# Decoding feed-forward weights in an attention stage: four half tiles in every chunk, and v^T e placed behind the scores

## The chip, the cores and the metric

One core of one Trainium2 chip runs the whole program. The metric is the device time of one execution in microseconds (us); the time of a kernel is the median of its runs. The core's engines are named as the profile names them: PE (TensorE matmuls), PEld (TensorE weight loads), DVE (VectorE), ACT (ScalarE), POOL (GpSimd) and SP (the queue that issues the transfers here).

## The reference

Three stages follow one another; 4 batches, 8 heads, 576 positions, head size 64, so 2304 rows of width 512.

```python
scores = scale * q @ k^T                       # 576 x 576 per head
scores = where(scores >= max(scores) - tau, scores, -1e9)
attn = exp(scores - max) / (sum + 1e-9)
x = (attn @ v), heads side by side             # 2304 x 512
h = ((x @ w1) * (x @ w2)) @ w3 @ w_out         # first feed-forward block
g = h @ w_in;  out = max(0.01 * g, g) @ w_out2 # second feed-forward block
```

q, k and v are float32. The weights are float64: the chip gets each as two 32-bit words and has to make float32 values of them, which is called decoding here.

## The kernel before

**Attention.** A unit is a pair of heads and one of two groups of query rows (256 rows or 320 rows). There are 32 units, in the order batch, group, pair. A unit of the first group has two chunks (128 query rows for both heads), one of the second group has three; the first of those three, written `None`, has 64 rows of both heads packed into one tile and counts with weight 1, all others with weight 2. That makes 80 chunks, `STEPS`, n = 0 to 79. Batch 0 group 0 is n = 0 to 7, batch 0 group 1 is n = 8 to 19.

One turn of the main loop (line 454 on) does, for chunk n: `mask(n)` (L239, DVE multiplies the exponentials by "score is over the threshold", two heads, and reads the one `sc` tile in PSUM); `scores(n + 1)` (L213 or L217 on PE into that same tile, then L223 maximum on DVE and L225 exponential on ACT, one head after the other); `transposes(n)` (L259 and L270 on PE, copied into `HH` by ACT at L274 and by DVE at L272, the last 64 keys into a tail tile `tl` by ACT at L277). In the first chunk of a unit `weighted` runs v^T e of the unit before (L292, 20 matmuls, from `tl` first and then from `HH`, copied out by ACT at L295); in the second `normalise` scales it (L320 and L322 on PE).

**Filling PE.** Between these pieces the loop puts matmuls of other work: `fill(0)`, `fill(1)` and `fill(2)` each run a share of `filler` (the first feed-forward block of a batch and group that is already done, `gated`, groups of 12 matmuls, L381 and L400) and at most one half of a fold. `fold_weights` multiplies w3 by w_out once, in 16 half folds of 4 column sums (L359). A half fold may only run when the weights that it reads have been decoded before this chunk began: `8 + 2 * (folded // 2) + 2 <= decoded`. At n = 9 the loop turns to `gated` for batch 0 group 0: it runs what is left of the folds at once, and `filler` is busy from n = 10 on.

**Decoding.** `stream` loads and decodes the weights in halves of a tile (128 x 512 words). There are 40 of them for the attention stage: 8 of `wo`, 16 of `w3` and 16 of `w12` (the matrices of `gated`). A half takes two ACT instructions (L142 and L144, each pinned behind the ACT instruction traced before it), a shift on DVE (L145) and a sum on POOL (L148). A half of `w12` takes more: the ACT copy at L150, the sum at L151 and a difference at L153, every second one on DVE, the rest on POOL. The temporaries `t` and `lw` have two buffers each, `w3` has three tiles in use at a time, and `raw`, the loaded words, four.

`load_halves(k)` decodes the next k halves. Each chunk takes 1.2 halves per unit of weight, collected in `due_halves` (2 or 3 in a chunk of weight 2). Half of them are called behind `fill(0)`, the others at the end of the chunk. `gated` calls `load_halves(1)` for itself when a matrix that it needs is not there.

**Order.** PE and SP keep the order of the program. The order of DVE, ACT and POOL is chosen when the program is built, from a model of the times, except for the pinned instructions. So the place of a call in the loop sets PE's and SP's order, and for the others only what is wanted first.

```python
        fill(0)                        # L474
        load_halves(kh // 2)
        if weigh:
            weighted(*weigh.pop())
        pieces = transposes(n)
```

Of the kernel before, what the change touches and what calls it, by code (L numbers as in the profile page):

```python
# [39 lines left out]
def attention_gated_ffn(ctx: ExitStack, tc: tile.TileContext, qkv, tau, w3t, wout, w12, w2, out):  # L40
# [144 lines left out]
    def scale_unit(u):  # L185

        if u >= len(units):
            return
        g = units[u][1]
        qk = qk_t[u]  # L190
        q = qk[:, S:S + GROUPS[g][1]]
        tc.keep_in_program_order(
            nc.vector.tensor_scalar(out=q, in0=q, scalar1=scl, scalar2=None, op0=ALU.mult))
        if g:
            for a in range(2):
                o = a * D
                nc.gpsimd.tensor_copy(qz[u % 2][o:o + D, o:o + D], qk[o:o + D, S:S + D])
# [4 lines left out]
    def scores(n):  # L202

        pair, g, c = STEPS[n]
        u = units.index((pair, g))
        qk = qk_t[u]
        heads = range(1 if c is None else 2)
        sc = ps_a.tile([P, 2, 2, 512], F32, tag="sc", name="sc")
        for half in range(2):
            ks = slice(half * HS, half * HS + HS)  # L210
            for a in heads:
                if c is None:
                    nc.tensor.matmul(sc[:, a, half, :HS], qz[u % 2], qk[:, ks], start=True, stop=True)  # L213
                else:
                    r = slice(a * D, a * D + D)
                    o = S + Q0[c] - GROUPS[g][0]
                    nc.tensor.matmul(sc[:, a, half, :HS], qk[r, o:o + P], qk[r, ks], start=True, stop=True)  # L217
        e = apool.tile([P, 2, S], F32, tag="e", name="e", bufs=2)
        ths = []
        for a in heads:  # L220
            nm = apool.tile([P, 1], F32, tag="nm", name="nm", bufs=4)
            th = apool.tile([P, 1], F32, tag="th", name="th", bufs=4)
            nc.vector.tensor_reduce(out=nm, in_=sc[:, a, :, :HS], op=ALU.max, axis=AX.XY, negate=True)  # L223
            nc.vector.tensor_scalar(out=th, in0=nm, scalar1=-1.0, scalar2=cb, op0=ALU.mult, op1=ALU.add)
            nc.scalar.activation(  # L225
                e[:, a].rearrange("p (a b) -> p a b", a=2), sc[:, a, :, :HS], AF.Exp, bias=nm)
            ths.append(th)
        sc_t[n], e_t[n] = (sc, ths), e

    def mask(n):  # L230
        pair, g, c = STEPS[n]
        sc, ths = sc_t.pop(n)
        key = (pair, g)
        if key not in stat:
            stat[key] = apool.tile([P, 5], F32, tag="stat", name="stat", bufs=4)
        for a, th in enumerate(ths):
            ev = e_t[n][:, a].rearrange("p (a b) -> p a b", a=2)
            o = 4 if c is None else 2 * (c % 2) + a
            nc.vector.scalar_tensor_tensor(  # L239
                out=ev, in0=sc[:, a, :, :HS], scalar=th, in1=ev, op0=ALU.is_ge, op1=ALU.mult,  # L240
                accum_out=stat[key][:, o:o + 1])
# [3 lines left out]
    def transposes(n):  # L245

        pair, g, c = STEPS[n]  # L250
        if (pair, g) not in he_t:
            he_t[pair, g] = apool.tile([P, 4, 2, 320], F32, tag="HH", name="HH")
        HH, tail = he_t[pair, g], tl[pair % 2]
        e = e_t.pop(n)
        tq = ps_a.tile([P, 2, P], F32, tag="tq", name="tq")
        if c is None:
            tp = ps_a.tile([P, 4, P], F32, tag="tp", name="tp")
            for kc in range(4):
                nc.tensor.transpose(tp[:, kc], e[:, 0, kc * P:kc * P + P], ident)  # L259
            nc.tensor.transpose(tq[:, 0], e[:, 0, S - P:], ident)  # L260
            nc.scalar.copy(HH[:, :, :, :D], tp.rearrange("p k (a w) -> p k a w", a=2))
            nc.vector.tensor_copy(
                tail[D:, :, :D], tq[D:, 0].rearrange("p (a w) -> p a w", a=2))
            yield
            return
        o = Q0[c] - GROUPS[g][0]
        for a in range(2):
            tp = ps_a.tile([P, 4, P], F32, tag="tp", name="tp")
            for kc in range(4):
                nc.tensor.transpose(tp[:, kc], e[:, a, kc * P:kc * P + P], ident)  # L270
            if a:
                nc.vector.tensor_copy(HH[:, :, a, o:o + P], tp)  # L272
            else:
                nc.scalar.copy(HH[:, :, a, o:o + P], tp)  # L274
            nc.tensor.transpose(tq[:, a], e[:, a, S - P:], ident)
            if a:
                nc.scalar.copy(tail[D:, :, o:o + P], tq[D:])  # L277
            yield
# [3 lines left out]
    def weighted(pair, g):  # L282

        gw = GROUPS[g][1]
        vv = vv_t[units.index((pair, g))]
        HH, tail = he_t.pop((pair, g)), tl[pair % 2]
        av = ps_w.tile([P, 512], F32, tag="w", name="av")
        for i in range(NK):
            for a in (1, 0):
                kc = (4, 0, 1, 2, 3)[i]  # L290
                rhs = (HH[:, kc, a] if kc < 4 else tail[:, a])[:, :gw]
                nc.tensor.matmul(  # L292
                    av[a * D:a * D + D, :gw], vv[:, a, kc], rhs, start=(i == 0), stop=(i == NK - 1))
        xs = apool.tile([P, 320], F32, tag="xs", name="xs", bufs=2)
        nc.scalar.copy(xs[:, :gw], av[:, :gw])  # L295
        xs_t[pair, g] = xs
# [133 lines left out]
    def load_halves(k):  # L430
        for _ in range(k):
            if next(loads, 0) != 0:
                halves_in[0] += 1

    def run(gen, k):
        for _ in range(k):
            if next(gen, 0) == 0:
                return

    def fold_some(most, halves):  # L440

        while most and folded[0] < 2 * KF and 8 + 2 * (folded[0] // 2) + 2 <= halves:
            next(folding, 0)
            folded[0] += 1
            most -= 1
# [1 line left out]
    folding = fold_weights()  # L447
    scores(0)
    weigh, norm = [], []
    due_halves = 0.0  # L450
    filler = iter(())
    queue = []
    rate, due = 0.0, 0.0
    for n in range(NS):
        pair, g, c = STEPS[n]
        u = units.index((pair, g))
        weight = 1 if c is None else 2
        last_of_unit = STEPS[(n + 1) % NS][:2] != (pair, g)
        decoded = halves_in[0]
        mask(n)  # L460
        if last_of_unit:
            scale_unit(u + 1)
        if n + 1 < NS:
            scores(n + 1)
        due += rate * weight
        k = int(due)
        due -= k
        parts = [(k + 2) // 3, (k + 1) // 3, k // 3]
        due_halves += 1.2 * weight
        kh = int(due_halves)  # L470
        due_halves -= kh

        def fill(i):
            run(filler, parts[i])  # L474
            fold_some(1, decoded)

        fill(0)
        load_halves(kh // 2)
        if weigh:
            weighted(*weigh.pop())  # L480
        pieces = transposes(n)
        next(pieces)
        fill(1)
        for _ in pieces:
            pass
        if norm:
            normalise(*norm.pop())
        if last_of_unit:
            reciprocals(pair, g)
            weigh.append((pair, g))  # L490
        elif u and STEPS[n - 1][:2] != (pair, g):
            norm.append(units[u - 1])
        fill(2)
        if n == 0 or STEPS[n - 1][:2] != (pair, g):
            load_unit(u + 2)
        load_halves(kh - kh // 2)
        if last_of_unit and pair % 4 == 3:
            queue.append((n + 2, pair // 4, g))
        if queue and queue[0][0] == n:
            _, b, gg = queue.pop(0)  # L500
            while halves_in[0] < 26:
                load_halves(1)
            fold_some(2 * KF, 24)
            next(folding, 0)
            for _ in filler:
                pass
            if (b, gg) == (0, 0):
                s_ld.close()
                gpool = s_ffn.enter_context(tc.tile_pool(name="gpool", bufs=8, reuse_waits="tile"))
                fpool = s_ffn.enter_context(tc.tile_pool(name="fpool", bufs=2, reuse_waits="tile"))  # L510
            if (b, gg) == (0, 1):
                while halves_in[0] < 40:
                    load_halves(1)
                in_order.close()
            filler = gated(b, gg)
            rate, due = (1.22, 1.55)[gg], 0.0
# [142 lines left out]
```

## Time and profile before

| | us |
|---|---|
| median of 3 runs (lowest, highest) | 1117.37 (1116.86, 1119.27) |
| the profiled execution, its own time | 1118.05 |
| its span, from the first to the last instruction | 1116.2 |
| PE busy in the span | 1062.5 (95%) |
| DVE, ACT, POOL busy | 499.6, 475.2, 262.6 |

The span is the time between the first and the last instruction that the profile saw; 1.85 us of the execution lie around it. The share of busy time is a mean over stages that differ much. The attention stage is cut here into chunks: the scores of chunk n + 1 are the first thing that PE does in turn n, so the start of `scores(n + 1)` marks the start of turn n on PE. In the profiled execution these starts are 13.20 (n = 0), 21.23, 28.55, 37.01, 44.48, 52.16, 61.71, 76.85, 89.53, 100.77 (n = 9) and 125.34 (n = 10).

### The profile page before, as it was taken

The numbers are of one execution on the slowest core, as the hardware profiler recorded it, in microseconds if no ns is written. First come the engines' busy times: TensorE is split into PE (matmuls) and PEld (weight loads), VectorE is DVE, ScalarE is ACT, GpSimd is POOL, SyncE is SP. The second block draws the span as 40 slices with busy tenths as digits, with TensorE's granted clock in tenths as the row PEclk, the third lists the DMA queues.
The fourth block names the chain that finished last, engine by engine and source line by source line (L and its number), as shares of the span: only waits on it lengthen the run. The fifth ranks groups of instructions, "written<-read, shape, count | busy, mean of one in ns | idle before, by whom it ended". The sixth has DMA issues, their size and how long they took to land.

```text
span 1116.2 us, 16066 instructions
## 1 busy us (share of the span) xinstructions
PE 1062.5 (95%) x6288; PEld 856.3 (77%) x6288; DVE 499.6 (45%) x1055; ACT 475.2 (43%) x891; POOL 262.6 (24%) x288
## 2 busy tenths in 40 slices
PE   4799988899999999998999999999999999999998
PEld 2454567788887788787888889977888888888887
DVE  5754577555566554666555634265411211111111
ACT  3654776344344343444434444377522222222232
POOL 1433564112121121111121227377500000000000
PEclk9899999999999999999999999999999999999999
DMA  8661343211212121112111014256210010010010
GB/s 269 206 193 53 103 144 120 68 52 36 63 39 62 42 58 49 32 55 63 41 46 47 2 48 141 84 179 196 75 38 1 19 48 1 1 48 1 1 38 19
DMA packets 35099, 77.58 MB, mean 70 GB/s; under 512 B 4560, under 2 KB 19408, under 8 KB 32976
## 3 DMA queue, kind: packets, MB, share of 16 engines
q1 hardware_dynamic: 34880, 76.56, 21.8%
q8 instruction: 49, 0.80, 0.3%
q14 instruction: 26, 0.21, 0.1%
q10 hardware_dynamic: 144, 0.00, 0.0%
HBM read 67.11 MB, written 9.44 MB: 69 GB/s over the span
## 4 chain that ended last, share of the span: by engine, by line
PE 77%; issue 8%; ACT 5%; DVE 4%; POOL 2%; DMA 2%; SPq 0%; ACTq 0%; DVEq 0%; POOLq 0%
PE po L596 16%; PE ps L574 16%; PE psab L381 14%; PE psh L400 9%; PE av L292 6%; PE sc L217 6%; PE ps L359 5%; PE tp L270 4%; PE sc L213 2%; DVE e L239 2%; ACT t L142 1%; DMA st<-in_w 1%; ACT e L225 1%; POOL gt L392 1%; ACT lw L144 1%
## 5 line engine op out<-in xcount | busy, mean ns | idle before, releaser
L381 PE MATMUL psab<-x,w 128*128 128x256 f32 (+1 forms) x1536 | 239.7, 307 | 3.7 <-ACT at L387 1.9
L381 PEld LDWEIGHTS psab<-x,w 128*128 128x128 f32 x1536 | 213.4, 192 | 22.7 <-issue 14.2
L574 PE MATMUL ps<-h,w 128*128 128x512 f32 (+1 forms) x960 | 215.7, 370 | 0.6 <-DVE h L550 0.3
L596 PE MATMUL po<-w,gg 128*128 128x512 f32 x864 | 213.8, 392 | 1.8 <-ACT gg L581 1.8
L574 PEld LDWEIGHTS ps<-h,w 128*128 128x128 f32 x960 | 169.0, 188 | 36.5 <-POOL w L153 1.3
L596 PEld LDWEIGHTS po<-w,gg 128*128 128x128 f32 x864 | 159.3, 188 | 38.3 <-ACT gg L581 3.5
L582 DVE TENSOR_TENSOR gg<-gf,gg 128x512 fp32r<-128x512 f32 (+1 forms) x80 | 61.2, 765 | 270.1 <-ACT gg L581 268.5
L225 ACT ACTIVATE e<-sc,nm 128x576 f32<-128x576 f32 x144 | 107.0, 743 | 131.7 <-DVE nm L223 131.5
L223 DVE TENSOR_REDUCE nm<-sc 128x1 f32<-128x576 f32 x144 | 108.9, 756 | 118.4 <-PE sc L217 68.9
L579 ACT ACTIVATE gf<-ps 128x512 f32<-128x512 f32 (+1 forms) x80 | 44.3, 555 | 227.0 <-PE ps L574 227.0
L239 DVE SCALAR_TENSOR_TENSOR e<-sc,th,e 128x576 f32<-128x576 f32 x144 | 112.6, 816 | 43.2 <-ACT e L225 43.1
L400 PE MATMUL psh<-gt,w 128*128 128x256 f32 (+1 forms) x768 | 115.2, 301 | 0.6 <-ACT ht L407 0.5
L217 PE MATMUL sc<-qk 64*128 64x288 f32 x512 | 85.3, 454 | 28.4 <-DVE e L239 20.0
L400 PEld LDWEIGHTS psh<-gt,w 128*128 128x128 f32 x768 | 104.1, 189 | 7.4 <-issue 5.1
L392 POOL TENSOR_TENSOR gt<-at,gt 128x256 fp32r<-128x256 f32 (+1 forms) x64 | 52.7, 823 | 238.2 <-ACT gt L391 238.2
L270 PE MATMUL tp<-ident,e 128*128 128x128 f32 x512 | 80.1, 280 | 7.3 <-ACT HH L274 7.3
L217 PEld LDWEIGHTS sc<-qk 64*128 64x128 f32 x512 | 47.1, 197 | 49.0 <-issue 15.5
L270 PEld LDWEIGHTS tp<-ident,e 128*128 128x128 f32 x512 | 60.6, 143 | 21.7 <-issue 11.6
L151 POOL TENSOR_TENSOR lw<-t,lw 128x512 int32<-128x512 int32 x48 | 64.9, 1357 | 39.4 <-ACT lw L144 24.5
L292 PE MATMUL av<-HH,vv 128*64 128x256 f32 (+1 forms) x512 | 69.5, 415 | 0.0
L551 POOL TENSOR_TENSOR h<-hr,h 128x1024 fp32r<-128x1024 f32 (+1 forms) x10 | 23.8, 2381 | 188.1 <-DVE h L550 188.1
L145 DVE TENSOR_SCALAR t<-t 128x512 int32<-128x512 int32 x72 | 48.1, 670 | 29.2 <-ACT t L142 28.9
(70 smaller groups left out, 965.3 us busy)
## 6 DMA issues: line engine op xcount, KB each, us to landing
st<-in_w SPq DMA_DIRECT2D x40, 512.0 KB, 4.5
vv<-in_qkv SPq DMA_DIRECT2D x64, 160.0 KB, 2.3
raw<-in_w3t SPq DMA_DIRECT2D x8, 1024.0 KB, 5.2
qk<-in_qkv SPq DMA_DIRECT2D x32, 208.0 KB, 3.7
qk<-in_qkv SPq DMA_DIRECT2D x32, 144.0 KB, 2.8
out<-os SPq DMA_DIRECT2D x18, 256.0 KB, 2.2
raw<-in_wout SPq DMA_DIRECT2D x4, 1024.0 KB, 10.1
raw<-in_w SPq DMA_DIRECT2D x4, 1024.0 KB, 7.1
```

Of the source, the lines that this page charges most:

```text
L151: nc.gpsimd.tensor_tensor(out=lw, in0=t, in1=lw, op=ALU.add)
L217: nc.tensor.matmul(sc[:, a, half, :HS], qk[r, o:o + P], qk[r, ks], start=True, stop=True)
L223: nc.vector.tensor_reduce(out=nm, in_=sc[:, a, :, :HS], op=ALU.max, axis=AX.XY, negate=True)
L225: nc.scalar.activation(e[:, a].rearrange("p (a b) -> p a b", a=2), sc[:, a, :, :HS], AF.Exp, bias=nm)
L239: nc.vector.scalar_tensor_tensor(out=ev, in0=sc[:, a, :, :HS], scalar=th, in1=ev, op0=ALU.is_ge, op1=ALU.mult, accum_out=stat[key][:, o:o ...
L270: nc.tensor.transpose(tp[:, kc], e[:, a, kc * P:kc * P + P], ident)
L292: nc.tensor.matmul(av[a * D:a * D + D, :gw], vv[:, a, kc], rhs, start=(i == 0), stop=(i == NK - 1))
L381: nc.tensor.matmul(ps[:, :gw], w12_t[i][:, a, mat * 512 + kk * P:mat * 512 + kk * P + P], xt[kk][:, c, :gw], start=(m == 0), stop=(m == 11))
L392: nc.gpsimd.tensor_tensor(out=gt[i][:, 1, :gw], in0=at[:, :gw], in1=f(gt[i][:, 0, :gw]), op=ALU.subtract)
L400: nc.tensor.matmul(ps[:, :gw], w34_t[i // 2][:, a, i % 2, o * P:o * P + P], gt[i][:, c, :gw], start=(m == 0), stop=(m == 23))
L574: nc.tensor.matmul(ps[:, :tw], w2_t[j][:, a, kk * P:kk * P + P], h3_t[ci][:, c, kk, :tw], start=(m == 0), stop=(m == 11))
L596: nc.tensor.matmul(po_t[t], gg[:, c, t * P:t * P + P], w2_t[j][:, a, 512:], start=(j == 0 and (a, c) == PASSES[0]), stop=(j == KF2 - 1 and ...
```

## The change

The count of halves becomes constant: two in the first chunk, four in every later one until there are none left. Half of them are called at the very start of the turn, in front of `mask(n)`; the other half stays at the end. `weighted` moves to the place directly behind `scores(n + 1)`, and `fill(0)` behind it.

```diff
@@ main loop, in front of it
-    due_halves = 0.0
@@ one turn
         decoded = halves_in[0]
+        kh = 2 if n == 0 else 4
+        load_halves(kh // 2)
         mask(n)
         if last_of_unit:
             scale_unit(u + 1)
         if n + 1 < NS:
             scores(n + 1)
@@
-        due_halves += 1.2 * weight
-        kh = int(due_halves)
-        due_halves -= kh
@@
-        fill(0)
-        load_halves(kh // 2)
         if weigh:
             weighted(*weigh.pop())
+        fill(0)
         pieces = transposes(n)
```

The halves decoded before chunk n begins become 0, 2, 6, 10, 14, 18, 22, 26, 30, 34, 38 for n = 0 to 10 (before, some 2.4 in each chunk, and 26 by the end of n = 9).

## Rows read from the trace of the kernel before

**Rows 1.** The page, parts 1 and 2: busy time, and PE's share in 40 slices.
```profile
PE 1062.5 (95%) x6288; PEld 856.3 (77%) x6288; DVE 499.6 (45%) x1055; ACT 475.2 (43%) x891; POOL 262.6 (24%) x288
...
PE   4799988899999999998999999999999999999998
```

**Rows 2.** Stretches: from:to, length, busy time (instructions) of each engine, PEclk, DMA, GB/s.
```profile
13.20:21.23 8.03, 4.88 (x18) 3.10 (x19) 4.43 (x11) 4.51 (x8) 0.00 (x0) 1.00 1.02 368
...
37.01:44.48 7.47, 2.92 (x21) 1.96 (x21) 6.28 (x14) 6.86 (x13) 4.02 (x5) 1.00 0.49 161
44.48:52.16 7.68, 6.58 (x38) 3.77 (x39) 5.39 (x15) 4.09 (x8) 3.28 (x4) 0.78 0.96 254
52.16:61.71 9.55, 9.55 (x38) 4.97 (x37) 5.09 (x12) 5.35 (x10) 3.53 (x3) 1.00 0.52 195
61.71:76.85 15.14, 15.14 (x63) 7.62 (x63) 8.93 (x20) 8.66 (x16) 7.02 (x8) 1.00 0.52 140
76.85:89.53 12.68, 12.68 (x41) 6.35 (x39) 3.84 (x8) 3.71 (x7) 2.60 (x3) 1.00 0.55 191
89.53:100.77 11.24, 11.24 (x50) 5.41 (x49) 5.69 (x12) 5.18 (x9) 2.53 (x2) 1.00 0.25 72
100.77:125.34 24.57, 23.43 (x69) 11.15 (x69) 12.86 (x24) 13.82 (x24) 12.47 (x13) 1.00 0.23 84
```

**Rows 3.** Stretches of the stage with gated filler, batch 0 and batch 1.
```profile
125.34:149.35 24.01, 19.37 (x142) 15.39 (x140) 18.13 (x38) 18.29 (x35) 13.36 (x13) 1.00 0.40 126
149.35:174.82 25.47, 20.81 (x142) 17.05 (x142) 19.02 (x39) 19.22 (x38) 16.33 (x17) 0.93 0.49 148
174.82:219.00 44.18, 40.36 (x292) 32.41 (x292) 28.48 (x65) 21.95 (x42) 10.74 (x13) 0.96 0.28 84
292.27:311.11 18.84, 18.63 (x144) 15.29 (x142) 11.40 (x27) 8.72 (x17) 2.21 (x5) 1.00 0.17 50
311.11:329.95 18.84, 18.63 (x141) 15.29 (x141) 12.28 (x31) 9.12 (x18) 4.43 (x8) 1.00 0.15 41
329.95:371.40 41.45, 38.29 (x291) 31.10 (x291) 25.88 (x64) 18.25 (x35) 6.38 (x10) 1.00 0.17 50
219.00:224.00 5.00, 5.00 (x24) 3.69 (x26) 2.29 (x5) 1.36 (x3) 0.86 (x1) 0.66 0.18 49
```

**Rows 4.** Waits of PE, 0 to 60 us: us in total, times, longest.
```profile
PE sc L217 <- DVE e L239: 10.0, 3, 4.9
PE sc L217 <- DVE qk L193: 8.3, 2, 6.0
```

**Rows 5.** Waits of PE, 125.34 to 219 us.
```profile
PE sc L217 <- DVE e L239: 4.8, 4, 1.8
PE sc L213 <- POOL qz L197: 4.2, 2, 2.1
```

**Rows 6.** Groups of ACT, 0 to 125.34 us: count, busy us, mean ns, idle before.
```profile
L142 ACT ACTIVATE t<-raw 128x512 f32<-128x512 f32 x26 | 17.4, 667 | 0.9 <-POOL w L148 0.7
L144 ACT ACTIVATE lw<-raw 128x512 int32<-128x512 uint32 x26 | 17.3, 665 | 0.0
```

**Rows 7.** Instructions that touch tile t, to 225 us: ns min/median/max.
```profile
L145 DVE TENSOR_SCALAR t<-t x40: 411/428/1244, 21.1 to 183.0; 128x512 int32<-128x512 int32 x40
```

**Rows 8.** Groups of POOL, 0 to 125.34 us.
```profile
L148 POOL TENSOR_TENSOR w<-t,lw 128x512 int32<-128x512 int32 x16 | 20.3, 1267 | 32.7 <-ACT lw L144 22.7 <-DVE t L145 4.9 <-DVE rr L303 4.0
```

**Rows 9.** Groups of ACT, 125.34 to 219 us.
```profile
L150 ACT CAST w<-t 128x512 fp32r<-128x512 f32 x14 | 8.7, 621 | 3.1 <-DVE t L145 3.0
```

**Rows 10.** Instructions of line 153: ns min/median/max.
```profile
L153 POOL TENSOR_TENSOR w<-lw,w x24: 1269/1360/1743, 119.9 to 791.1; 128x512 fp32r<-128x512 f32 x24
```

**Rows 11.** Timeline, 154 to 160 us: start, us, engine, instruction.
```profile
156.03 0.69 DVE L272 COPY HH<-tp 128x512 f32<-128x512 f32 x1
...
156.48 0.37 ACT L277 COPY tl<-tq 64x256 f32<-64x256 f32 x1
...
157.20 0.50 PE L381 MATMUL psab<-x,w 128*128 128x256 f32 x2
```

## The prediction

> **What bounds the kernel now.** The page comes first: PE is busy 95% of the span, and its row of 40 slices shows where it is not: in the first two slices, about slices 6 to 8, and thinly later [rows 1]. A change that moves no matmul away can only win where PE stands idle or runs at its lower clock, so the next view is the table of stretches, cut by chunks. In the first turns PE works 4.88 of 8.03 us and 2.92 of 7.47 us [rows 2]; from the turn that has its first half folds (52.16 us, n = 5) to 111 us it is full. The waits say why the first turns are long: the next scores wait for the masks of the chunk before, and for a scaling of q behind them on DVE [rows 4]. That is a chain of latencies (scores, maximum, exponential, maximum, exponential, two masks), and PE has nothing to put into it until weights are decoded.
>
> The second loss is in 125 to 219 us, where `gated` has begun and the 14 last halves are decoded beside it. Batch 1 does the same work later with nothing to decode, and so gives the price: three stretches of 24.01, 25.47 and 44.18 us against 18.84, 18.84 and 41.45 us [rows 3], together 93.66 against 79.13. **14.5 us hang on these 14 halves, 1.04 us on each**, the low clock that follows the waits (0.93 and 0.96 granted) included. The waits show it as scores that wait for DVE's masks and for the `qz` copy, which stands behind the decoding on POOL [rows 5].
>
> **The change part by part.** The number of decoding instructions, matmuls and transfers stays the same; all moves earlier.
>
> *Half folds.* By the counts of halves, two fit in turn 3, three in each of turns 4 to 7 and two in turn 8: all 16 are done by then. Before, they were 2, 3, 3, 2 and 6 in turns 5 to 9. I price a turn by the row of a turn with the same contents [rows 2]: 9.55 (two half folds), 15.14 (three and v^T e), 12.68 (three), 11.24 (turn 8, two). Turns 3 to 8 become 9.55 + 15.14 + 12.68 + 15.14 + 12.68 + 11.24 = 76.4 us. Turn 9 now has neither folds nor `gated` work: PE runs dry and the turn lasts as its chain or its decoding. The chain alone is some 7.5 us (7.47 and 7.68 of the turns without folds). Its four halves of `w12` take longer: one half passes 0.67 + 0.67 on ACT [rows 6], 0.43 on DVE [rows 7], 0.62 on ACT [rows 9] and 1.27 + 1.36 on POOL [rows 8, 10], 5.0 us in all, and two buffers let two pass at a time, so 2.5 us each. Four make 10.0 us, which I take; the ends are 7.5 and 13. Turns 3 to 9 then sum to 86.4, against 88.3 before (37.01 to 125.34): **-1.9 us** (-4.4 to +1.1). The six half folds of turn 9 were not idle time before, which is why folding early wins so little.
>
> *Decoding in the first turns.* In turns 0 to 3 nothing fills PE, so what delays the masks delays all. ACT has the room: before, it works 4.5 of 8.0 us in turn 0 and 6.9 of 7.5 in turn 3 [rows 2], and the two halves in front of the mask start where the last exponential ends, while DVE masks and PE scores. The cost is on DVE: the shift of the first such half is ready while the first of the two masks runs, and is wanted first, so I put one shift of 0.43 us between the masks of four turns: **+1.7 us** (0 if they go behind, +5.0 if each lasts the 1.24 us that is the longest shift in the trace [rows 7]).
>
> *Crowding in turns 6 to 8.* `w3` has three tiles, so the sum of half 22 must wait for a fold in turn 6 itself; six halves then want to pass in turn 7, 15 us at 2.5 us each, in a turn of 12.7. What waits behind them on POOL is the `qz` copy for chunk 8, and PE's scores wait for that; such a wait was 2.1 us at its longest [rows 5]. I take **+1.5 us** (0 to +4).
>
> *Clock.* After the dry turn the matmuls run at the lower of the two levels for a while. The row to go by is 219 to 224 us, behind a wait of 1.8 us [rows 5]: granted clock 0.66, a mix of 1.2 and 2.4 GHz, so 0.34 x 5.0 = **1.7 us** (0 to 2) [rows 3]. The Trainium skill ("TensorE: Matmul & The Clock Gate", "HAM oscillation") has it that idle gaps throttle the engine again; the trace agrees with its 0.66.
>
> *The stage of `gated`.* 38 halves have been called by the end of turn 9, and two are left for turn 10. With two more still in the queue, four of the 14 are decoded there: 4 x 1.04 = 4.2 us of the 14.5 stay, **-10.4 us** (-14.5 if none, -7.3 if half of them).
>
> *v^T e behind the scores.* PE's contents of a turn are the same, in another order. It reads the tail and `HH` sooner by one `fill(0)`, and what covers the copies is then the scores alone. In the tightest place that I found, no filler behind the last transposes, the copies end at 156.72 and 156.85 us and the scores give way at 157.20 [rows 11]: **0**, in all 32 units. If the cover fell short by 0.1 us each it would be +3. Earlier reads also release v's buffers sooner, for which SP waits; those loads are a unit ahead, and I count no gain.
>
> *SP.* The loads of raw words are issued in front of the mask rather than behind `fill(0)`, so ahead of the next unit's loads; in the first turn transfers fill the DMA engines (share 1.02 [rows 2]), and by turn 3 they are half idle (0.49). Seven halves are loaded ahead: 0.
>
> Sum: -1.9 + 1.7 + 1.5 + 1.7 - 10.4 = **-7.4 us**. The profiled execution took 1118.05 us, so 1110.65; the median of the runs shown lies 0.68 lower, so I predict **1110.0 us**.
>
> **The rivals.** *Masks behind shifts (slower).* If both shifts of the front half stand ahead of the masks in DVE's order, and each meets a POOL sum and lasts 1.24 us instead of 0.43, a turn without filler loses 2.5 us. There are six (0 to 3, 9 and 10): +14.9 in place of +1.7, in all +5.8, **1123 us**. It decides from four of these turns on (9.1 / 2.5). For it: the shift comes first in the program, and shifts of 1.24 us exist. Against it: the median is 0.43 [rows 7], and the shift cannot start before ACT's first pass (0.67), by which time a mask is running. The Trainium skill ("SBUF — State Buffer", "Who interferes with whom") speaks against the change here: a DVE `tensor_scalar` that uses both ports and a GpSimd instruction lock each other out for a whole instruction. By it every shift that meets a sum would be a long one, and the time this rival's; the trace has both kinds, mostly short ones.
>
> *The decoding doesn't stay ahead.* Seven of the 14 halves are left over, and crowding costs 4: -1.9 + 1.7 + 4 + 1.7 - 7.3 = -1.8, **1115.6 us**, no change that can be told. For it: three `w3` tiles, two buffers, and 2.5 us a half. Against it: turns 6 to 8 are long (39 us).
>
> *The dry turn costs nothing.* Turn 9 takes 7.5 us, the crowding and the clock nothing, and nothing is left over: +1.7 - 4.4 - 14.5 = -17.2, **1100 us**.
>
> *v^T e waits for the copies.* If DVE's copy into `HH` slips behind a mask, each of 32 units waits about 0.5 us: +16, **1126 us**. Against it: the scores in front wait for the same masks.
>
> **How the numbers follow.** Forecast 0.62, decoding not ahead 0.11, dry turn for nothing 0.15, masks behind shifts 0.09, v^T e waiting 0.03. A measurement of this kernel can tell some 0.2%, 2.2 us, from no change. The forecast's own ends give nearly always a gain over that, the fourth case too; the third splits between gain and none: faster 0.79, same 0.11, slower 0.10. The range goes down to the 1100 us of the dry-turn case and up to 1116.5, a little beyond the decoding that doesn't stay ahead; the two slow cases and the outer tail are left out.
>
> **What would show it.** Right: half folds (L359) in turns 3 to 8 and none in one burst; stretches of about 19 to 21 us between the `None` scores where 24.01 and 25.47 stood; a turn 9 of 8 to 12 us with PE idle, and a dip of the clock behind it; turns 0 to 2 longer by about half a microsecond each. Wrong: turns 0 to 3 longer by 2 us and more, with shifts ahead of the masks in the timeline of DVE; PE waiting in L292 for L272 or L277; or the stretches of `gated` as long as before, with L142 still in them.

## The result, and the profile after

The changed kernel takes **1107.34 us**, the median of 4 runs (1105.86 to 1109.01), against 1117.60 for the kernel before in the same session (4 runs). The ratio is 0.9907, 95% interval 0.9889 to 0.9925: about 10 us faster, where 7.4 were forecast. The profiled execution has a span of 1105.6 us; the one before had 1116.2, so the two traces have 10.6 us between them.

The page first, parts 1 and 2, busy time and PE's 40 slices; it answers to [rows 1].

```profile
PE 1054.3 (95%) x6288; PEld 853.5 (77%) x6288; DVE 500.4 (45%) x1055; ACT 472.8 (43%) x891; POOL 264.2 (24%) x288
...
PE   4899699899999999998999999999999999999998
```

Instruction counts are those of before on every engine: the work only moved. Slices 2, 6 and 7 are fuller, and one slice of 6 has appeared, the fifth, at 111 to 138 us. The page says no more than that; the stretches do. The columns are those of [rows 2], and the cuts are again the starts of `scores(n + 1)` on PE: turns 1 to 3, turn 9, the three stretches of the gated stage, ten microseconds around the start of that stage, and one later batch, from the last packed scores of batch 2 to those of batch 3. The last line is the same stretch of the trace before.

```profile
21.22:29.82 8.60, 4.88 (x19) 3.04 (x19) 6.80 (x15) 5.67 (x10) 4.53 (x4) 1.00 0.71 253
29.82:39.71 9.89, 7.98 (x39) 4.43 (x39) 6.39 (x14) 5.74 (x11) 5.09 (x4) 1.00 0.69 206
39.71:52.50 12.79, 11.31 (x36) 5.56 (x36) 6.64 (x16) 7.22 (x14) 5.10 (x4) 0.87 0.66 229
...
119.31:130.73 11.42, 2.92 (x21) 1.96 (x20) 9.60 (x21) 10.31 (x20) 8.19 (x8) 0.74 0.54 158
130.73:153.88 23.15, 20.84 (x141) 17.01 (x141) 16.91 (x33) 14.48 (x28) 12.82 (x13) 0.91 0.52 157
153.88:172.59 18.71, 18.50 (x141) 15.29 (x142) 12.30 (x31) 9.00 (x18) 4.42 (x8) 1.00 0.14 41
172.59:213.72 41.13, 37.98 (x291) 31.05 (x291) 25.87 (x64) 18.02 (x35) 6.38 (x10) 1.00 0.18 51
125.00:135.00 10.00, 4.27 (x15) 3.70 (x16) 8.15 (x18) 8.34 (x16) 8.75 (x11) 0.50 0.65 201
...
473.43:623.12 149.69, 146.06 (x1084) 123.95 (x1084) 87.78 (x213) 65.03 (x128) 27.24 (x44) 1.00 0.15 42
...
482.62:633.45 150.83, 147.26 (x1084) 123.84 (x1084) 87.81 (x213) 65.67 (x128) 27.21 (x44) 1.00 0.14 42
```

Laid beside the cuts of before [rows 2, 3], every microsecond of the 10.6 has a place. The last column is the prediction's sum, cut in the same way.

| stretch | before | after | difference | forecast |
|---|---|---|---|---|
| turns 0 to 2 | 23.81 | 26.51 | +2.7 | +1.3 |
| turn 3 | 7.47 | 12.79 | +5.3 | +2.5 |
| turns 4 to 8 | 56.29 | 66.81 | +10.5 | +12.1 |
| turn 9 | 24.57 | 11.42 | -13.2 | -14.6 |
| gated stage of batch 0 | 93.66 | 82.99 | -10.7 | -8.7 |
| all behind it | 897.2 | 891.9 | -5.3 | 0 |

So turn 10 starts **5.4 us later** than before (130.73 against 125.34), and all of the gain, and more, comes behind that point. In the gated stage the ACT groups show how little decoding is left, five copies of `w12` halves where there were 14 [rows 9]:

```profile
L150 ACT CAST w<-t 128x512 fp32r<-128x512 f32 x5 | 3.0, 615 | 1.4 <-DVE t L145 1.4
```

**Turns 0 to 2.** The timeline of DVE (start, length, instruction, and in brackets the idle time before it and what ended it) shows where the shifts L145 went. The scores of these turns began at 21.22 and 29.82 us.

```profile
23.69 0.79 DVE L145 TENSOR_SCALAR t<-t 128x512 int32<-128x512 int32 x1 [0.49 <-ACT t L142]
24.40 0.74 DVE L223 TENSOR_REDUCE nm<-sc 128x1 f32<-128x576 f32 x1
...
33.53 1.25 DVE L145 TENSOR_SCALAR t<-t 128x512 int32<-128x512 int32 x1 [0.45 <-ACT t L142]
34.70 0.74 DVE L223 TENSOR_REDUCE nm<-sc 128x1 f32<-128x576 f32 x1
```

They stand neither in front of the masks nor between them, but behind them, in front of the next maximum. In turn 2 the maximum begins 4.88 us after its scores; in the kernel before it was 2.34 us (scores at 28.55):

```profile
30.89 0.76 DVE L223 TENSOR_REDUCE nm<-sc 128x1 f32<-128x576 f32 x1 [1.57 <-PE sc L217]
```

DVE stands idle for 0.45 us in front of the second shift, waiting for ACT, although the scores have been there since 32.1 us: its order was chosen when the program was built, and in it the shift comes first. Turn 2 as a whole grows by 1.4 us and not by 2.5, because before the change PE was still busy with v^T e and the transposes when the masks were done.

**Turn 3.** The first half fold could not start until POOL had summed the half that it reads, and then ran at the lower clock: 5.40 us for eight matmuls that take 3.60 a little later (timeline of PE and POOL).

```profile
41.10 1.27 POOL L148 TENSOR_TENSOR w<-t,lw 128x512 int32<-128x512 int32 x1 [4.91 <-ACT lw L144]
42.43 5.40 PE L359 MATMUL ps<-wo,w 128*128 128x512 f32 x8 [1.48 <-POOL w L148]
48.21 3.60 PE L359 MATMUL ps<-wo,w 128*128 128x512 f32 x8
```

**Turn 9** is the dry one, with PE busy for 2.92 of 11.42 us. Its chain can be followed through the timeline of ACT, DVE, POOL and PE:

```profile
122.19 0.65 ACT L144 ACTIVATE lw<-st 128x512 int32<-128x512 uint32 x1
122.74 0.57 ACT L274 COPY HH<-tp 128x512 f32<-128x512 f32 x1
123.21 0.74 ACT L225 ACTIVATE e<-sc,nm 128x576 f32<-128x576 f32 x1
...
125.98 0.74 ACT L225 ACTIVATE e<-sc,nm 128x576 f32<-128x576 f32 x1
...
126.76 0.82 DVE L239 SCALAR_TENSOR_TENSOR e<-sc,th,e 128x576 f32<-128x576 f32 x1
...
128.50 1.35 POOL L153 TENSOR_TENSOR w<-lw,w 128x512 fp32r<-128x512 f32 x1
129.80 0.88 POOL L197 COPY qz<-qk 64x64 f32<-64x64 f32 x2
...
130.73 2.29 PE L213 MATMUL sc<-qk,qz 128*128 128x288 f32 x4 [6.39 <-POOL qz L197]
132.41 2.95 PE L381 MATMUL psab<-x,w 128*128 128x256 f32 x12
```

ACT decodes a half (L142 from 121.62, L144) in front of the `HH` copy and the exponential, so the masks begin at 126.76. They are over at 128.3, but PE waits until 130.7: the `qz` copy for the packed chunk stands on POOL behind a difference of `w12` (L153). The scaling of q on DVE (L193) is over at 128.7, so POOL holds the copy up for 1.1 us; the scaling, 0.4 us behind the masks, and the copy itself, 0.9 us, make up the rest. Then scores and filler run at about half speed; the granted clock is 0.50 over 125 to 135 us, the lower level (1.2 of 2.4 GHz).

**Behind the stage.** One unit of batch 1 now takes 18.71 us where it took 18.84 [rows 3]. The PE timeline of the stretch around v^T e, before:

```profile
316.22 1.24 PE L217 MATMUL sc<-qk 64*128 64x288 f32 x8
317.39 1.69 PE L381 MATMUL psab<-x,w 128*128 128x256 f32 x12
319.01 0.76 PE L292 MATMUL av<-tl,vv 128*64 128x320 f32 x4
...
321.85 0.66 PE L259 MATMUL tp<-ident,e 128*128 128x128 f32 x4
...
322.55 1.24 PE L217 MATMUL sc<-qk 64*128 64x288 f32 x8
```

and after:

```profile
310.16 1.24 PE L217 MATMUL sc<-qk 64*128 64x288 f32 x8
311.33 0.76 PE L292 MATMUL av<-tl,vv 128*64 128x320 f32 x4
...
314.17 1.70 PE L381 MATMUL psab<-x,w 128*128 128x256 f32 x12
315.71 0.60 PE L259 MATMUL tp<-ident,e 128*128 128x128 f32 x4
...
316.35 1.24 PE L217 MATMUL sc<-qk 64*128 64x288 f32 x8
```

From scores to scores it is 6.33 us before and 6.19 after, with the same matmuls. The part of the array that a matmul uses stands in its row (64\*128, 128\*128, 128\*64). Before, it changes four times: at the filler, at v^T e, at the transposes, at the scores. After, it changes three times, because filler and transposes, both 128\*128, stand next to each other. What such a change does is seen in the weight loads of the same stretch (PEld, after):

```profile
314.17 1.49 PEld L381 LDWEIGHTS psab<-x,w 128*128 128x128 f32 x12 [0.49 <-issue]
315.61 0.46 PEld L259 LDWEIGHTS tp<-ident,e 128*128 128x128 f32 x4
```

The first load of the filler starts with its matmuls at 314.17, after 0.49 us without any load, and waits for nothing that the trace shows (issue). The first load of the transposes, with no change in front of it, starts at 315.61, 0.10 ahead of its matmul. The Trainium skill ("TensorEngine Tiling (Array Packing)", "Key Properties") has it that a change of the tiling mode drains the engine; the trace agrees, and gives it a size, 0.14 us.

### The profile page after: what moved, and what is told of

Same layout as the page of the kernel before. It is cut to its first block, busy times and chain, and to the rows that moved or that the text cites. A ratio compares the mean times of both kernels' runs of the same rounds, so it can differ in the third digit from the quotient of the medians.

```text
span 1105.6 us, 16076 instructions
## 1 busy us (share of the span) xinstructions
PE 1054.3 (95%) x6288; PEld 853.5 (77%) x6288; DVE 500.4 (45%) x1055; ACT 472.8 (43%) x891; POOL 264.2 (24%) x288
## 4 chain that ended last, share of the span: by engine, by line
PE 76%; issue 9%; ACT 5%; DVE 4%; POOL 3%; DMA 2%; ACTq 0%; SPq 0%; DVEq 0%; POOLq 0%
PE po L593 16%; PE ps L571 16%; PE psab L381 13%; PE psh L400 9%; PE av L292 5%; PE ps L359 5%; PE sc L217 5%; PE tp L270 4%; PE sc L213 2%; DVE e L239 1%; DVE t L145 1%; POOL gt L392 1%; ACT t L142 1%; PE tq L275 1%; ACT lw L144 1%
## 5 line engine op out<-in xcount | busy, mean ns | idle before, releaser
L381 PE MATMUL psab<-x,w 128*128 128x256 f32 (+1 forms) x1536 | 236.2, 304 | 0.7 <-ACT at L387 0.7
L381 PEld LDWEIGHTS psab<-x,w 128*128 128x128 f32 x1536 | 210.7, 190 | 19.6 <-issue 15.9
L292 PE MATMUL av<-HH,vv 128*64 128x256 f32 (+1 forms) x512 | 69.0, 413 | 0.0
L145 DVE TENSOR_SCALAR t<-t 128x512 int32<-128x512 int32 x72 | 50.1, 698 | 26.6 <-ACT t L142 26.4
```

The costliest lines, as they stand in the source:

```text
L292: nc.tensor.matmul(av[a * D:a * D + D, :gw], vv[:, a, kc], rhs, start=(i == 0), stop=(i == NK - 1))
L381: nc.tensor.matmul(ps[:, :gw], w12_t[i][:, a, mat * 512 + kk * P:mat * 512 + kk * P + P], xt[kk][:, c, :gw], start=(m == 0), stop=(m == 11))
```

## Experiments

The runs fell into three sessions, each on one chip with its own runs of the kernel before: 1116.79 us (17 runs) for the first four, 1117.13 (11) for the next four, 1116.56 (15) for the last three. Ratios are against these.

### The order alone

The kernel before, with v^T e put behind the scores and the decoding left as it was.

```diff
-        fill(0)
-        load_halves(kh // 2)
         if weigh:
             weighted(*weigh.pop())
+        fill(0)
+        load_halves(kh // 2)
```

> Only the second half of the change: v^T e directly behind the scores, decoding as before. Theory (each unit's turn gets some 0.13 us shorter because a group of matmuls with full weights now stands between v^T e and the transposes, read from units of 25.23 and 18.84 us before and 25.07 and 18.71 us after): 32 units, about 4 us less than the kernel before, some 1113.5 us. Rival (the 5.3 us that the profile after lies ahead behind 219 us are differences of the granted clock alone): the same as before, 1117 to 1118 us.

1115.91 us, ratio 0.9989 (0.9978 to 1.0000), 12 runs. A unit of batch 1 takes 18.71 us, as in the changed kernel, but the gated stage of batch 0 is as long as before, 93.88 against 93.66 us (stretch, columns as above):

```profile
125.57:219.45 93.88, 79.46 (x574) 64.82 (x572) 64.36 (x142) 58.83 (x112) 40.84 (x43) 0.96 0.36 112
```

In that stage PE's waits for the masks (four, 6.1 us in all) can swallow the 0.14 us of a unit: a PE that waits for those gains nothing from being done sooner. Behind it the trace does hold the gain, 149.68 us for a batch against 150.83. But the first turn behind a batch's last unit took 13.06 us at a granted clock of 0.76 (520.52 to 533.58 us) where the same turn takes 10.05 us one batch earlier, which is nearly as much as three batches gain. The saving in a unit is shown; in the median some 1 us of it can be seen, less than was expected.

### The decoding alone

The changed kernel, with v^T e back behind `fill(0)`.

```diff
-        if weigh:
-            weighted(*weigh.pop())
         fill(0)
+        if weigh:
+            weighted(*weigh.pop())
```

> Only the first half of the change: four halves per turn, half of them in front of the mask, v^T e behind fill(0) as before. Theory (decoding brings 10.7 us in the stage of gated and gives 5.4 us back in turns 0 to 9; the order brings the rest): 1111 to 1112.5 us, with units of 18.8 us and not 18.7 behind turn 10. Rival (the order brings nothing): 1107 us, as with the whole change.

1111.40 us, ratio 0.9954 (0.9940 to 0.9968), 6 runs. Turn 10 starts at 129.64, a unit takes 18.85 us and a batch 150.84, as before the change. The decoding by itself is worth some 5 us. By the ratios the two parts alone bring 5.1 and 1.2 us, together less than the 10.4 of the whole change; this gap is not closed (see what stays open, below).

### The qz copy called one turn earlier

`scale_unit` (scaling of q on DVE, `qz` copy on POOL) of a unit with a packed chunk is called in the turn before, so that it is not behind that turn's decoding.

```diff
+        to_pack = u + 1 < len(units) and units[u + 1][1] == 1
-        if last_of_unit:
+        if last_of_unit and not to_pack:
             scale_unit(u + 1)
         if n + 1 < NS:
             scores(n + 1)
+        if to_pack and not last_of_unit and STEPS[(n + 2) % NS][:2] != (pair, g):
+            scale_unit(u + 1)
```

> The whole change, but the next unit's q is scaled and packed into qz one turn earlier, so that this copy stands on POOL ahead of the sums of the last halves. Theory (turn 9 lasts 11.4 us because the packed copy stands behind the decoding): the 6.4 us wait of the scores for qz is gone, turn 9 becomes 7.5 to 9 us, and the time 2 to 4 us less than with the change, 1103.5 to 1105.5. Rival (the masks and the other copies of that turn are as late, being behind decoding too): the wait changes its name and the time stays at 1107.

1102.36 us, ratio 0.9868 (0.9852 to 0.9884), 4 runs. Turn 9 falls from 11.42 to 9.32 us (stretches):

```profile
119.11:128.43 9.32, 2.92 (x21) 1.99 (x21) 7.62 (x18) 9.17 (x18) 6.18 (x7) 0.77 0.48 164
```

Its PE waits still have one before the packed scores:

```profile
PE sc L213 <- POOL lw L151: 4.3, 1, 4.3
```

The releaser named is a POOL sum, which the scores don't read; what ends at that moment on DVE is the second mask, at 128.3. So scaling and copy in their old place cost 2.1 us, and the masks are late next; in the timeline they follow an exponential that stands behind the decoding on ACT. A unit with a packed chunk is 0.47 us shorter too, 18.24 us: a wait for `qz` of 0.2 to 0.3 us stood in each, one that the kernel before has as well; the other half of the 0.47 was not traced.

### Two half folds kept for the dry turn

```diff
         def fill(i):
             run(filler, parts[i])
-            fold_some(1, decoded)
+            if (n, i) not in ((7, 2), (8, 1), (8, 2)):
+                fold_some(1, decoded)
```

> The whole change, but two half folds are kept back from turns 7 and 8 for turn 9. Theory (what turn 9 loses is that PE has nothing to do there): turns 7 and 8 get shorter by 3.4 us each, turn 9 stays near 11 us, in all 4 to 7 us less than with the change, 1100.5 to 1103.5. Rival (turns 7 to 9 last as long as their twelve halves take, 2.5 us each and more): turn 9 grows by what 7 and 8 lose, 1106 to 1108.

1102.28 us, ratio 0.9872 (0.9856 to 0.9889), 5 runs. Turns 7 to 9 and the ten microseconds around the start of the gated stage:

```profile
94.00:103.24 9.24, 9.24 (x33) 4.94 (x31) 6.26 (x11) 7.27 (x14) 7.76 (x6) 1.00 0.59 205
103.24:112.45 9.21, 7.73 (x42) 4.11 (x42) 6.57 (x15) 8.61 (x17) 7.41 (x7) 1.00 0.90 280
112.45:123.75 11.30, 9.62 (x36) 5.04 (x36) 10.61 (x21) 9.74 (x18) 9.50 (x9) 1.00 0.51 159
125.00:135.00 10.00, 7.84 (x58) 5.85 (x60) 8.57 (x16) 9.09 (x18) 8.23 (x10) 1.00 0.69 211
```

Turn 9 is as long as without them, 11.30 us, now with PE busy for 9.62 of it: the half folds cost nothing there (the filler waits 0.24 us for their result), and turns 7 and 8 take 18.45 us instead of the 23.77 between 95.54 and 119.31 in the changed kernel. The granted clock stays at 1.00 where it was 0.50. Turn 10 starts at 123.75, 7.0 us sooner; 1.5 us of that were there before the edit acts (turn 7 starts at 94.00 against 95.54), and 5.4 lie in turns 7 to 9. This trace is of the fastest of the five executions; by the ratios the edit is worth 4.5 us. The unit behind turn 9 takes 22.5 us instead of 23.15. The changed kernel folds too early: the dry turn is of its own making.

### The changed kernel again

The changed kernel itself, in the second session, for the next three to be read against.

> The whole change once more, beside the others of this call, as the point of comparison: 1105.5 to 1108.5 us by either theory, with turn 10 starting near 130.7 us.

1107.59 us, ratio 0.9912 (0.9896 to 0.9928), 5 runs; turn 10 starts at 131.23 us in its trace.

### The front half of the decoding in its old place

```diff
-        load_halves(kh // 2)
         mask(n)
@@
         fill(0)
+        load_halves(kh // 2)
```

> The whole change, but the first half of each turn's halves is called where it stood before, behind v^T e and fill(0), and no longer in front of the mask. Theory (the place hardly matters, because ACT, DVE and POOL take the halves when a temporary is free, and the amount per turn is what counts): within 2 us of the whole change. Rival (the place in front of the mask uses the time in which ACT waits for the next scores, and is worth the 1 to 2 us per turn in turns 0 to 3): 4 us slower or more, turn 4 starting behind 54 us instead of at 52.5.

1109.20 us, ratio 0.9928 (0.9912 to 0.9944), 6 runs. That is 1.6 us over the changed kernel, and the intervals overlap. In the trace turn 4 starts at 54.96, as the rival had it and 2.5 us later than in the changed kernel, but turn 10 at 131.39, 0.2 to 0.7 us behind it. Where the call stands matters little here; that there are four halves per chunk is what counts.

### Two halves per chunk in turns 0 to 2

```diff
-        kh = 2 if n == 0 else 4
+        kh = 2 if n < 3 else 4
```

> The whole change, but two halves in each of turns 0 to 2 and four from turn 3 on. Half folds then start in turn 4 and two are left for turn 9. Theory (decoding four halves in the turns that have nothing else costs there 2.7 us and 3.2 more in turn 3, and what it brings forward, the folds, only leaves turn 9 dry): turns 0 to 2 back to 23.8 us, turn 10 starting at 122 to 125 us; four more halves are then decoded beside gated at 1.04 us each; in all 2 to 5 us less than the whole change. Rival (decoding from the first chunk on is what brings the gain): 2 us slower than the whole change or more.

1110.15 us, ratio 0.9938 (0.9924 to 0.9952), 6 runs: 2.6 us slower than the changed kernel, where 2 to 5 us faster had been my theory. Turns 0 to 2 and the gated stage:

```profile
13.19:36.34 23.15, 16.48 (x74) 10.05 (x74) 15.17 (x36) 11.68 (x20) 6.90 (x6) 1.00 0.75 254
126.69:216.23 89.54, 77.86 (x573) 63.15 (x573) 60.65 (x136) 49.57 (x97) 32.06 (x38) 0.98 0.32 93
```

The first turns do get back their length (23.15 us; 26.51 with four halves, 23.81 before), and turn 10 starts 4.0 us sooner than in the changed kernel. But in the gated stage nine copies of halves are left, against five:

```profile
L150 ACT CAST w<-t 128x512 fp32r<-128x512 f32 x9 | 5.6, 619 | 3.0 <-DVE t L145 2.9
```

and it takes 89.54 us against 82.99, 6.5 us for four halves, 1.6 each. Decoding in the chain of the first turns is dear, in the gated stage dearer.

### Both repairs together

The edits of the qz copy and of the kept folds in one kernel.

> Both cures together: two half folds kept for turn 9, and the next unit's q packed a turn earlier. Theory (they are separate losses: PE without work in turn 9, and the packed copy behind other work on POOL, there and 0.2 to 0.5 us in each later unit of the second group): the two gains of some 4 us each add up to 7 or 8, 1098 to 1100.5 us. Rival (both cure the same wait in turn 9): as the better one alone, 1102 us.

**1099.16 us**, ratio 0.9835 (0.9812 to 0.9857), 5 runs (1093.82 to 1101.43). The two had given 4.9 and 4.5 us by their ratios against 0.9912, together 9.4; the ratio now is 8.6 us under the changed kernel. They add up nearly, and this is the best version found. What is left of the decoding shows in the first unit of the gated stage:

```profile
121.82:146.07 24.25, 20.46 (x142) 16.85 (x143) 19.30 (x40) 16.46 (x32) 14.52 (x15) 0.93 0.54 163
```

against 18.24 for such a unit with nothing to decode. Its granted clock of 0.93 is a dip: 0.66 over 125 to 130 us, behind a wait of the filler of 1.63 us that the trace puts down to the last half fold's result (L365 on DVE). So the half folds in turn 9 are not free in every version.

### v^T e in two pieces

To test the change of shape by itself, v^T e is cut into 8 and 12 matmuls with `fill(0)` between: two changes more in every unit, the same matmuls.

```diff
         for i in range(NK):
+            if i == 2:
+                between()
             for a in (1, 0):
@@
-            weighted(*weigh.pop())
-        fill(0)
+            weighted(*weigh.pop(), between=lambda: fill(0))
+        else:
+            fill(0)
```

> The whole change, but v^T e is cut into 8 and 12 matmuls with fill(0) between them. Theory (what the order brings is one change less between matmuls on 64 columns and matmuls on 128 columns of the array: the next weights are then loaded only when the last matmul has ended, 0.1 us each): two changes more per unit with a filler, 0.2 to 0.3 us each in 28 units, units of 18.9 to 19.0 us instead of 18.71, in all 6 to 8 us slower than the whole change. Rival (the order helps because PE waits less for copies): the first part waits as before, units stay at 18.7 us and the time within 1 us.

A unit of batch 1 (PE timeline; stretch underneath):

```profile
313.36 0.71 PE L294 MATMUL av<-HH,vv 128*64 128x320 f32 x4
314.00 1.69 PE L383 MATMUL psab<-x,w 128*128 128x256 f32 x12
315.62 1.84 PE L294 MATMUL av<-HH,vv 128*64 128x320 f32 x12
```

```profile
306.49:325.50 19.01, 18.80 (x142) 15.22 (x142) 12.31 (x31) 9.00 (x18) 4.42 (x8) 1.00 0.14 41
```

19.01 us. With 18.85 for the old order and 18.71 for the new, that makes steps of 0.16 and 0.14 us for one change more each time. The whole is slower by more than these steps: 1117.25 us, ratio 1.0005 (0.9994 to 1.0015), 11 runs, some 10 us over the changed kernel, where 32 units at 0.30 make 9.6 at most. A batch of its trace takes 153.66 us against 149.67, 4.0 more, of which eight units make 2.4. The rest is the granted clock: the first turn behind a batch's last unit is slow in all three batches of this trace, 11.92 us at 0.86 against 10.35 us for the same turn of the next pair.

```profile
367.24:379.16 11.92, 11.92 (x74) 9.31 (x75) 5.46 (x14) 4.15 (x8) 1.58 (x2) 0.86 0.24 68
```

The trace of the changed kernel has one such dip and this one three, so some 3 of the 10 us are the clock and some 7 (24 units at 0.30) the order. Whether the dips come with this order or by chance was not tested.

### The best version with the old order

The kernel of both repairs, with v^T e behind `fill(0)` again.

```diff
-        if weigh:
-            weighted(*weigh.pop())
         fill(0)
+        if weigh:
+            weighted(*weigh.pop())
```

> Both cures (half folds kept, q packed early), but v^T e behind fill(0) as before the change. Theory (the order is worth 0.14 us in each unit in which PE is full, in all some 4 us, as between the whole change and the decoding alone): 4 us slower than with both cures, about 1103 us. Rival (it is worth only the 1 us that it brought alone): 1099.5 to 1100.5 us.

1100.39 us, ratio 0.9852 (0.9839 to 0.9866), 4 runs. By the traces the old order costs 1.18 us per batch (149.88 against 148.70); the medians are 1.2 us apart in all, which is the rival's figure: the traces show the 0.14 us per unit, the medians less.

### Four w3 tiles

The kernel of both repairs, with a fourth tile for `w3`.

```diff
-tag=tag, name=name, bufs=3)
+tag=tag, name=name, bufs=4)
```

> Both cures and four tiles of w3 instead of three. Theory (the sums of the last w3 halves wait for folds in turn 6, and the halves of w12 that are left for turns 10 and 11 for that): the sums at L148 no longer wait for PE in turn 6, turns 10 to 12 (24.3 us with both cures, 18.24 without decoding) get 1 to 3 us shorter, 1096 to 1098.5 us. Rival (two temporaries per half are the limit, not the tiles): 1099 us, and turns 10 to 12 stay at 24 us.

1100.28 us, ratio 0.9843 (0.9818 to 0.9869), 5 runs, no difference. The first unit of the gated stage takes 24.17 us, against 24.25. The waits that the fourth tile was to remove did go: with three tiles POOL stands idle in front of the sums (L148) for 9.1 us in two waits for PE, with four tiles in none. So the three tiles do hold the sums up, as the prediction had it, but in the kernel of both repairs that is not what limits.

## Why the prediction came out right, and which steps did not

The sign, the place of the gain and the range were right (1107.34 in 1100 to 1116.5), and the time is 2.7 us under the forecast. That is nearer than its parts deserve, and in part luck, because errors of either sign cancel: the work in front of turn 10 came out 4.1 us longer than forecast, the gated stage 2.0 and the rest 5.3 us shorter.

- **The gated stage, right.** Four halves left over at 1.04 us were forecast; five copies stand there, and the stage is 10.7 us shorter, against 10.4 less 1.7 for the clock. That batch 1 prices what decoding costs batch 0 [rows 3] held, though a left-over half can cost 1.6 us, as the run with two halves in the first turns shows.
- **Turns 4 to 8, right by their rows.** 66.88 from turns with the same contents [rows 2], 66.81 measured. Folding early wins nothing there, as said. The crowding of 1.5 us in turns 6 to 8 did not come: their sum is 38.75 us, their price without it 39.06. It came in turn 9, and its mechanism was in part the forecast's, the `qz` copy behind decoding on POOL, for 1.1 us: with scaling and copy a turn earlier, turn 9 is 2.1 us shorter.
- **Turn 9, 1.4 us short.** 10.0 was the decoding's own rate; measured 11.42, of which scaling and copy in their place are 2.1. The rate itself was taken a little high: it has every difference on POOL, where every second one runs on DVE (0.69 us). What I did not see is that the dry turn could be filled for nothing with half folds held back from turns 7 and 8.
- **Turns 0 to 2, half the size and another place.** "One shift of 0.43 us between the masks" was wrong: the shifts go behind the masks and hold up the next maximum on DVE, and beside a POOL sum they last up to 1.25 us. 2.7 us instead of 1.3, all of it in turns 1 and 2. The slow rival had the long shifts right and their place wrong; it was not reached.
- **Turn 3, the step that failed.** I priced it at 9.55 by a turn whose two half folds were ready at its start. My count of halves was of halves called, not of halves summed: the fold waits 1.48 us for POOL, and the first one runs at the lower clock behind that idle time, 1.8 us more. The turn's granted clock is 0.87. The size differs between executions: in nine traces with these calls of the decoding the wait for POOL is always there (0.57 to 1.49 us), but in four of them the first fold takes 3.70 us and the turn 11.5, in five 5.2 to 5.8 and the turn 12.8 to 13.2.
- **The clock behind the dry turn, right in kind.** 1.7 us forecast; the first unit's granted clock of 0.91 over 23.15 us makes 2.1 by the same estimate. With PE kept busy in turn 9 the dip was gone in one trace, but in the trace of both repairs it is back (0.66 over 125 to 130 us), behind a wait of 1.63 us.
- **v^T e at 0, wrong.** "PE's contents of a turn are the same, in another order" left out that the order sets how often the array changes its shape. One change fewer is 0.14 us in each unit with filler, shown by three orders. The copies were in time, as forecast, but for two waits of L292 for L277, 1.0 us in all (before, one of 0.5).

The 5.3 us behind the stage are then 1.14 per batch (150.83 to 149.69), 3.4 for the three batches that are left, and some 1.6 of clock: the profiled execution of before dipped at the start of two batches (48.14 us from 219.00, and the first line below, against 46.57 us one batch later, the second line), that of after at the start of one (47.60 us from 213.72, against 46.11).

```profile
371.40:419.50 48.10, 48.10 (x335) 41.20 (x335) 26.21 (x64) 20.23 (x40) 9.82 (x14) 0.96 0.19 50
524.07:570.64 46.57, 46.57 (x335) 39.80 (x335) 26.21 (x64) 20.12 (x40) 9.84 (x14) 1.00 0.18 52
```

**What stays open** is how much of the order's gain a median holds. Three pairs of ratios give 1.2 us (0.9989), 4.7 to 5.2 (0.9954 against 0.9907 and 0.9912) and 1.9 (0.9852 against 0.9835), each with an interval of 1 to 3 us either way; the trace says 3.4. Dips of the granted clock where one batch ends and the next begins differ between the traces, none to three of them at 1.5 to 3 us each, and are as large as what is to be measured. Why they come in one execution and not in another was not tested.

## What to carry to other kernels

Price a turn by a row with the same contents, and ask of its inputs when they are finished, not when they were called for. When work is moved to an earlier place, look for the place that it leaves empty: here two half folds held back were nearly free in the turn that had run dry, and worth nearly half as much again as the whole change. And where an engine is full, count what its order itself costs: matmuls of one shape side by side saved 0.14 us each time here, with no work moved away.

## What the runs showed of the hardware

- A change of the array's shape between matmuls (64\*128, 128\*128, 128\*64) costs PE 0.14 to 0.16 us, and the weight load behind it starts with its matmul instead of 0.10 us ahead: units of 18.71, 18.85 and 19.01 us with one change more each time.
- A shift on DVE (`tensor_scalar`, 128x512 int32) takes 0.41 us by itself and up to 1.49 us beside a POOL sum. The Trainium skill ("SBUF — State Buffer", "Who interferes with whom") names the lock between the two for which the prediction weighed its slow rival; the long shifts agree with it. By the Trainium skill, in the same section, whichever of the two issues first holds the shared ports. So a shift that meets a sum need not be a long one, as the prediction had it. The chain lost only what stood in front of a maximum.
- After 6.4 us of waiting PE ran its next matmuls at about half speed (2.95 us for a group that takes 1.67 to 1.80); with half folds in the wait the granted clock stayed at 1.00 over the same ten microseconds. A later wait of 1.63 us, in the version with both repairs, was followed by a granted clock of 0.66 over five microseconds.
